# Attention block loop: the last weighted-value products issued before the third set of transposes, and the copy of their sum issued one iteration earlier

## The chip, the cores and the metric

The kernel runs on one core of a Trainium2 chip. The metric is the device time of one launch in microseconds (us), median of three runs. The engines are TensorE (PE, with its weight loads shown apart as PEld), VectorE (DVE), ScalarE (ACT), GpSimd (POOL) and SyncE (SP), which issues the DMAs.

## The reference

Three layers follow each other: a clustered attention, a bilinear layer and a gated layer. All inputs and outputs are float32.

```
q_assign = argmax(q_n . c_n);  k_assign = argmax(k_n . c_n)      # 16 clusters per head
scores   = q k^T / sqrt(64), masked to pairs of the same cluster
attn     = exp(scores - rowmax);  attn = attn / (rowsum + 1e-9)
x        = attn v                       # (2, 8, 768, 64) -> (1536, 512)
x        = ((x w1) * (x w2)) w3 w_out   # 512 -> 1024 -> 1024 -> 512
out      = (sigmoid(x w_gate) * (x w_val)) w_out2    # 512 -> 1536 -> 512
```

## The kernel before, in words

The attention runs over 16 heads as 8 pairs (`pr`), two heads (`e`) a pair and three groups of 256 queries (`q0`) a head: 48 blocks. One block goes through these steps, each of them a small function:

- `scores(j)`: for each half of the block (128 queries, j = 2i or 2i+1) four matmuls write 128 x 768 scores into PSUM (lines 312 to 315; pool `ps_s`, 2 buffers).
- `maxima(j)`: DVE takes the negated row maximum (`nm`, line 322). `exponentials(j)`: ACT writes exp(s + nm) to SBUF (`e`, line 333).
- `transposes(i, k2)`, k2 = 0, 1, 2: PE turns 256 of the 768 keys, four 128 x 128 transposes a set, into PSUM (`pt`, line 343; pool `ps_t`, 3 buffers).
- `split_hi` and `split_lo`: the turned weights are kept as a rounded part `ph` (ACT, line 361) and a remainder `pl` (DVE, line 372), which free the `pt` buffer. For half of the blocks the set k2 = 0 goes by ACT into `pc` (line 358), and POOL forms both parts.
- `weighted_v(i, k2)`: four matmuls (lines 384 and 385) add ph and pl times the values `vx` into `av`. The pool `ps_a` has a single buffer: one block's sum has to be copied out before the next block's first product may start.
- `take_x(i)`: ACT copies `av` into the pair's result `xa` (line 393).

The loop is software-pipelined: its iteration i issues scores for block i+1 or i+2, transposes for block i, and products for block i-1. From the start of the loop on, the instructions of PE, DVE, ACT, POOL and SP are issued in the order in which this code is written: there is no scheduler, and each engine takes its list from the front. `at` is the place of an iteration in its pair (0 to 5). Some iterations carry more: the preparation of the next pair (`prep_...`), the inverse of the row sums (`invert`, ACT line 407 and DVE line 408, at = 4) and its turn by PE (`turn_sums`, line 413, at = 5), and steps that convert the next layer's weights (`convert`; on ACT lines 93 and 94 or line 108), at the end of iterations at = 1 and 3, and in some pairs 5, of the pairs 1 to 6.

On PE an iteration is: four score matmuls, transposes 0, eight products (k2 = 0 and 1, of block i-1), four score matmuls, transposes 1, transposes 2, four products (k2 = 2). On ACT it is: `take_x(i-2)`, ph of set 2 of block i-1, ph or pc of set 0, an exponential, ph of set 1, a second exponential, and after it the conversion steps, if there are any.

After the attention the two matrix layers follow as one long list of matmuls (lines 65 to 67), with their evacuations attached. The last iterations of the attention, i = 47 to 49, drain it.

Of the kernel before, what the change touches and what calls it, by code (L numbers as in the profile page):

```python
# [27 lines left out]
def tile_cluster_attention__then__moe__then__gated_moe(  # L28
# [236 lines left out]
    def prep_code(pr):  # L265
        sm = opnd.pop((pr, "top"))
        lead(pr).tensor_tensor(out=sm, in0=sm, in1=dec.unsqueeze(1).broadcast_to([128, S // 32, C]), op=ALU.mult)
        opnd[pr, "code"] = sm
# [25 lines left out]
    def prep_v(pr, e):  # L294
        vx = core.tile([128, KT, 2, D], F32R, tag="vx", name=f"vx{pr}_{e}", bufs=3)
        split(raw[pr, "v"][:, e], vx[:, :, e, :], vx[:, :, 1 - e, :], nc.gpsimd, nc.gpsimd)
        opnd[pr, e, "v"] = vx
# [6 lines left out]
    def scores(j):  # L304

        if not 0 <= j < 2 * NB:
            return
        pr, e, q0 = blocks[j // 2]
        QH, KH, QX, KX = opnd[pr, e]
        q = slice(q0 + 128 * (j % 2), q0 + 128 * (j % 2) + 128)  # L310
        sp = ps_s.tile([128, 1024], F32, tag="s", name=f"s{j}")
        nc.tensor.matmul(sp[:, 0:512], QH[:, q], KH[:, 0:512], start=True, stop=False)
        nc.tensor.matmul(sp[:, 512:S], QH[:, q], KH[:, 512:S], start=True, stop=False)
        nc.tensor.matmul(sp[:, 0:512], QX[:, q], KX[:, 0:512], start=False, stop=True)
        nc.tensor.matmul(sp[:, 512:S], QX[:, q], KX[:, 512:S], start=False, stop=True)  # L315
        sps[j] = sp

    def maxima(j):
        if j not in sps:
            return  # L320
        nms[j] = core.tile([128, 1], F32, tag="nm", name=f"nm{j}", bufs=4)
        nc.vector.tensor_reduce(out=nms[j], in_=sps[j][:, 0:S], axis=AX.X, op=ALU.max, negate=True)  # L322
# [13 lines left out]
    def transposes(i, k2):  # L336
        if not 0 <= i < NB:
            return
        pt = ps_t.tile([128, 2, 256], F32, tag="t", name=f"pt{i}_{k2}")
        for kk in range(2):  # L340
            for t in range(2):
                k0 = 128 * (2 * k2 + kk)
                nc.tensor.transpose(pt[:, kk, 128 * t : 128 * t + 128], exps[2 * i + t][:, k0 : k0 + 128], ident)  # L343
        pts[i, k2] = pt

    def by_pool(i, k2):

        return k2 == 0 and i % 6 in (1, 2, 4)

    def split_hi(i, k2):  # L350
        if (i, k2) not in pts:
            return
        pt = pts[i, k2]
        ph = core.tile([128, 2, 256], F32R, tag="ph", name=f"ph{i}_{k2}", bufs=4)
        pl = core.tile([128, 2, 256], F32R, tag="pl", name=f"pl{i}_{k2}", bufs=4)
        if by_pool(i, k2):
            pc = core.tile([128, 2, 256], F32, tag="pc", name=f"pc{i}", bufs=1)
            nc.scalar.copy(pc, pt)
            pts[i, k2] = pc
        else:  # L360
            nc.scalar.copy(ph, pt)  # L361
        phs[i, k2] = (ph, pl)
# [11 lines left out]
    def weighted_v(i, k2):  # L374
        if not 0 <= i < NB:
            return
        pr, e, q0 = blocks[i]
        ph, pl = phs.pop((i, k2))
        if k2 == 0:
            avs[i] = ps_a.tile([128, 256], F32, tag="a", name=f"av{i}")  # L380
        for kk in range(2):
            kt = 2 * k2 + kk
            w = opnd[pr, e, "v"][:, kt].rearrange("p j d -> p (j d)")
            nc.tensor.matmul(avs[i], w, ph[:, kk, :], start=kt == 0, stop=False)  # L384
            nc.tensor.matmul(avs[i], w, pl[:, kk, :], start=False, stop=kt == KT - 1)  # L385

    def take_x(i):
        if i not in avs:
            return
        pr, e, q0 = blocks[i]  # L390
        if q0 == 0:
            acc_x[pr, e] = core.tile([128, S], F32, tag=f"xa{e}", name=f"xa{pr}_{e}", bufs=2 - e)
        nc.scalar.copy(acc_x[pr, e][:, q0 : q0 + 256], avs.pop(i))  # L393
# [16 lines left out]
    def turn_sums(pr):  # L410

        rp = ps_t.tile([128, 2, 256], F32, tag="t", name=f"rp{pr}")[0 : 2 * KT, 0, 0:128]
        nc.tensor.transpose(rp, acc_x.pop((pr, "sum")), ident)
        acc_x[pr, "rp"] = rp

    def store_sums(pr):
        rp = acc_x.pop((pr, "rp"))
        rt = core.tile([2 * KT, 128], F32, tag="rt", name=f"rt{pr}", bufs=1)
        nc.vector.tensor_copy(rt, rp)
        nc.sync.dma_start(r_dram[pr], rt)  # L420
# [85 lines left out]
    if True:  # L506
        for e in range(2):
            prep_v(0, e)
        for i in range(-2, NB + 2):
            pr, at = divmod(i, 6)  # L510
            nxt = pr + 1 if 0 <= i and pr + 1 < NPR else None
            later = nxt + 1 if nxt and nxt + 1 < NPR else None
            late = nxt == 1

            scores(2 * i + 3)
            take_x(i - 2)
            split_hi(i - 1, 2)
            transposes(i, 0)
            if i == NB - 1:
                turn_sums(pr)  # L520
            maxima(2 * i + 3)
            if i == NB - 1:
                store_sums(pr)
            if nxt and at == 1 + late:
                prep_code(nxt)
            if nxt and at == 1:
                prep_scatter(nxt, 1)
            if later and at == 0:
                load_qk(later)
            if at == 2 and 0 < pr and i < NB:  # L530
                join_x(pr - 1)
            split_lo(i - 1, 2)
            split_hi(i, 0)
            split_lo(i, 0)
            if nxt and at == 3:
                for e in range(2):
                    prep_mask(nxt, e)
            if 0 < pr and i < NB and at == 5:
                norm_x(pr - 1)
                split_x(pr - 1)  # L540
            if nxt and at == 2:
                prep_v(nxt, 0)
            if 0 < pr and i < NB and at == 3:
                add_x(pr - 1)
                spread(pr - 1, "xb", 1)
            exponentials(2 * i + 3)
            if later and at == 3:
                halves = prep_split(later)
                next(halves)
            if later and at == 4:  # L550
                for _ in halves:
                    pass
            weighted_v(i - 1, 0)
            weighted_v(i - 1, 1)
            if 0 <= i < NB - 1 and at == 5:
                turn_sums(pr)
            if i == 0:
                prep_scatter(1, 0)
            if later and at == 5:
                prep_scatter(later, 0)  # L560
            if at == 0 and pr < 4:
                convert(pr)

            scores(2 * i + 4)
            if nxt and at == 0 and not late or i == 1:
                prep_add(nxt)
            if 0 < pr < NPR and at == 0:
                prep_v(pr, 1)
            if nxt and at == 0:
                load_v(nxt)  # L570
            transposes(i, 1)
            split_hi(i, 1)
            transposes(i, 2)
            maxima(2 * i + 4)
            split_lo(i, 1)
            exponentials(2 * i + 4)
            weighted_v(i - 1, 2)
            if 0 <= i < NB and at == 4:
                invert(pr)
            if 0 <= i < NB - 1 and at == 5:  # L580
                store_sums(pr)
            if i == -2:
                halves = prep_split(1)
                next(halves)
            if i == -1:
                for _ in halves:
                    pass
            if i == 0:
                prep_sims(1)
                prep_sum(1)  # L590
            if nxt and at == late:
                prep_argmax(nxt)
            if nxt and at == 1 + late:
                prep_onehot(nxt)
            if nxt and at == 2:
                prep_turn(nxt)
            if (pr, at) in CONVERT:
                convert(CONVERT[pr, at])
            if later and at == 5:
                prep_sims(later)  # L600
                prep_sum(later)
            if i == NB - 2:
                end_move(0)
            if i == NB:
                end_move(1, FIRST)
                spread(END, "raw", 3)
                end_add(0)
        end_move(1, LAST)
        end_add(1, FIRST)
        end_norm(FIRST)  # L610
        end_split(FIRST)
        end_add(1, LAST)
        end_norm(LAST)
        end_split(LAST)
# [530 lines left out]
```

## Time and profile before

| | |
|---|---|
| median of 3 runs | 779.38 us (778.66 to 780.47) |
| the profiled execution, its own time | 780.68 us |
| its span, first to last instruction | 778.9 us |
| mean granted TensorE clock | 0.996 of full speed (2.4 GHz) |
| PE busy | 754.6 us (97%) |
| DVE, ACT, POOL busy | 575.4, 470.6, 410.8 us |
| first and last copy `xa<-av` of the attention | 32.66 and 254.19 us |
| first matmul of the layer after it | 253.99 us |

Times in the rows are counted from the start of the span. A row of the timeline gives start, duration, engine, line, operation, output and inputs. A bracket at its end gives the idle time of the engine before it and the instruction that ended it. Matmuls are pipelined, so the start of the next row, not the duration, tells how long one held the engine.

### The profile page before, as it was taken

The page shows a single profiled execution, that of the slowest core. Times are in us where ns is not written, and L with a number is a line of the kernel's source. Part 1 is how long each engine was busy: PE and PEld are TensorE (multiplying, and loading weights), DVE is VectorE, ACT ScalarE, POOL GpSimd, SP SyncE. Part 2 cuts the span into 40 slices and gives each one's busy share as a digit, 9 for nine tenths or more (in the row PEclk, how much of TensorE's full clock was granted, in tenths as well). Part 3 has the DMA queues.
Part 4 walks back from the last instruction along what each step waited for, and adds up shares of the span by engine and source line. Part 5 has one row for each costly group of instructions (what it writes and reads, how often), then busy time and mean ns, then how long its engine had stood idle before and what let it go on. Part 6 is the DMA issues. An engine that isn't in the chain of part 4 may idle for free.

```text
span 778.9 us, 12205 instructions
## 1 busy us (share of the span) xinstructions
PE 754.6 (97%) x4293; PEld 683.5 (88%) x4293; DVE 575.4 (74%) x895; ACT 470.6 (60%) x980; POOL 410.8 (53%) x418
## 2 busy tenths in 40 slices
PE   7999999998999999999999999899999999999998
PEld 7888888888988888888888999899999999999996
DVE  6798989898887566666673367658576877879674
ACT  3789788879787455546552244576756455564630
POOL 3447777776765256333241137474755647475520
PEclk9999999999999999999999999999999999999999
DMA  8867767666621534333340001130311213031004
GB/s 223 198 178 173 203 168 184 178 153 163 153 62 52 166 113 154 115 134 133 111 144 20 1 0 55 54 109 1 127 36 57 107 54 109 1 109 55 28 0 163
DMA packets 28893, 82.63 MB, mean 106 GB/s; under 512 B 4800, under 2 KB 4960, under 8 KB 28832
## 3 DMA queue, kind: packets, MB, share of 16 engines
q1 hardware_dynamic: 28832, 81.86, 35.7%
q8 instruction: 34, 0.56, 0.3%
q14 instruction: 27, 0.22, 0.1%
HBM read 52.49 MB, written 3.19 MB: 71 GB/s over the span
## 4 chain that ended last, share of the span: by engine, by line
PE 78%; DVE 6%; ACT 4%; issue 4%; DMA 3%; POOL 3%; SPq 2%; ACTq 0%; DVEq 0%; POOLq 0%
PE p L67 12%; PE p L66 12%; PE p L65 12%; PE p_a L65 4%; PE p_a L66 4%; PE p_a L67 4%; PE pt L343 4%; PE av L384 3%; PE av L385 2%; SPq L62 2%; PE p_b L65 2%; PE p_b L66 2%; PE p_b L67 2%; PE w34p L67 2%; PE w34p L65 2%
## 5 line engine op out<-in xcount | busy, mean ns | idle before, releaser
L322 DVE TENSOR_REDUCE nm<-s 128x1 f32<-128x768 f32 x96 | 90.3, 942 | 10.8 <-PE s L315 10.4
L333 ACT ACTIVATE e<-s,nm 128x768 f32<-128x768 f32 x96 | 87.4, 910 | 14.0 <-DVE nm L322 13.4
L384 PE MATMUL av<-ph,vx 128*128 128x256 f32 x288 | 80.6, 309 | 11.3 <-ACT xa L393 10.8
L372 DVE TENSOR_TENSOR pl<-pt,ph 128x512 fp32r<-128x512 f32 x120 | 80.0, 682 | 11.4 <-ACT ph L361 10.4
L361 ACT CAST ph<-pt 128x512 fp32r<-128x512 f32 x120 | 69.3, 594 | 23.4 <-PE pt L343 22.9
L343 PE MATMUL pt<-ident,e 128*128 128x128 f32 x576 | 79.8, 274 | 0.7 <-DVE pl L372 0.6
L65 PE MATMUL p<-x,w 128*128 128x512 f32 (+1 forms) x208 | 80.0, 385 | 0.0
L67 PE MATMUL p<-x,w 128*128 128x512 f32 (+1 forms) x208 | 80.0, 385 | 0.0
L66 PE MATMUL p<-x,w 128*128 128x512 f32 (+1 forms) x208 | 80.0, 385 | 0.0
L385 PE MATMUL av<-pl,vx 128*128 128x256 f32 x288 | 72.6, 281 | 0.0
L343 PEld LDWEIGHTS pt<-ident,e 128*128 128x128 f32 x576 | 67.3, 142 | 5.8 <-PE pt L343 0.9
L384 PEld LDWEIGHTS av<-ph,vx 128*128 128x128 f32 x288 | 54.3, 188 | 19.1 <-ACT xa L393 8.9
L106 POOL TENSOR_TENSOR w_a<-w_f 128x512 uint32<-128x512 uint32 x32 | 34.8, 1086 | 62.5 <-DVE w_f L105 28.6
L1024 DVE TENSOR_TENSOR acc<-p,acc 128x512 f32<-128x512 f32 x60 | 41.2, 687 | 29.9 <-PE p L67 29.5
L931 ACT COPY s<-p_a 128x384 f32<-128x384 f32 x72 | 34.4, 479 | 44.3 <-PE p_a L67 43.9
L855 POOL TENSOR_TENSOR wgv_a<-wgv_f 128x512 uint32<-128x512 uint32 x24 | 25.3, 1056 | 62.4 <-DVE wgv_f L854 43.7
L67 PE MATMUL p<-wo,u 128*128 128x512 f32 x144 | 57.0, 396 | 0.0
L66 PE MATMUL p<-wo,u 128*128 128x512 f32 x144 | 56.7, 394 | 0.0
L65 PE MATMUL p<-wo,u 128*128 128x512 f32 x144 | 56.0, 389 | 0.0
L385 PEld LDWEIGHTS av<-pl,vx 128*128 128x128 f32 x288 | 54.6, 190 | 0.1
L66 PEld LDWEIGHTS p<-x,w 128*128 128x128 f32 x208 | 39.1, 188 | 7.5
L67 PEld LDWEIGHTS p<-x,w 128*128 128x128 f32 x208 | 39.1, 188 | 7.5
(232 smaller groups left out, 2295.6 us busy)
## 6 DMA issues: line engine op xcount, KB each, us to landing
wgv_f<-in_w_gv_dram SPq DMA_DIRECT2D x24, 512.0 KB, 3.2
wo_f<-in_w_out_dram SPq DMA_DIRECT2D x20, 512.0 KB, 3.2
w_f<-in_w_dram SPq DMA_DIRECT2D x16, 512.0 KB, 4.3
w_f<-in_w3T_dram SPq DMA_DIRECT2D x16, 512.0 KB, 4.1
raw<-in_qkT_dram SPq DMA_DIRECT2D x16, 384.0 KB, 3.3
vraw<-in_v_dram SPq DMA_DIRECT2D x8, 384.0 KB
QH<-hi SPq DMA_DIRECT2D x16, 192.0 KB, 4.7
KH<-hi SPq DMA_DIRECT2D x16, 192.0 KB, 3.1
```

Source lines behind the costliest of these rows:

```text
L65: nc.tensor.matmul(ps, whi, xhi, start=start, stop=False, skip_group_check=more)
L66: nc.tensor.matmul(ps, whi, xlo, start=False, stop=False, skip_group_check=more)
L67: nc.tensor.matmul(ps, wlo, xhi, start=False, stop=stop, skip_group_check=more)
L106: nc.gpsimd.tensor_tensor(out=a, in0=high, in1=low, op=ALU.add)
L322: nc.vector.tensor_reduce(out=nms[j], in_=sps[j][:, 0:S], axis=AX.X, op=ALU.max, negate=True)
L333: nc.scalar.activation(et, sps.pop(j)[:, 0:S], AF.Exp, bias=nms.pop(j), accum_out=acc_x[pr, "sum"][:, at : at + 1])
L343: nc.tensor.transpose(pt[:, kk, 128 * t : 128 * t + 128], exps[2 * i + t][:, k0 : k0 + 128], ident)
L361: nc.scalar.copy(ph, pt)
L372: nc.vector.tensor_tensor(out=pl, in0=src, in1=ph, op=ALU.subtract)
L384: nc.tensor.matmul(avs[i], w, ph[:, kk, :], start=kt == 0, stop=False)
L385: nc.tensor.matmul(avs[i], w, pl[:, kk, :], start=False, stop=kt == KT - 1)
L1024: nc.vector.tensor_tensor(out=acc[:, t, :], in0=bk, in1=acc[:, t, :], op=ALU.add)
```

## The change

In each iteration of the attention loop the last four products of block i-1 (`weighted_v(i - 1, 2)`) move up on PE, from behind the transposes of set 2 of block i to in front of them. The copy of the finished sum moves on ACT from the head of the next iteration (`take_x(i - 2)` there) to the middle of the same one (`take_x(i - 1)`), behind the ph of set 1 and in front of the second exponential and of all that follows it.

```diff
             scores(2 * i + 3)
-            take_x(i - 2)
             split_hi(i - 1, 2)
             transposes(i, 0)
...
             transposes(i, 1)
             split_hi(i, 1)
+            weighted_v(i - 1, 2)
             transposes(i, 2)
+            take_x(i - 1)
             maxima(2 * i + 4)
             split_lo(i, 1)
             exponentials(2 * i + 4)
-            weighted_v(i - 1, 2)
             if 0 <= i < NB and at == 4:
                 invert(pr)
```

The lists of DVE, POOL and SP keep their order. Those of ACT and PE change in every iteration in the same way. ACT, in the iteration whose conversion steps are lines 93 and 94 (weights `w_1_0`; av_2259 is the sum of the block whose products end here, ph_2_2308 the last rounded part of the block after it), before:

```order
181 L333 ACTIVATE e_2257,ss_2050<-s_2223,nm_2237 128x768
182 L361 CAST ph_1_2278<-pt_1_2273 128x512
183 L333 ACTIVATE e_2289,ss_2050<-s_2268,nm_2286 128x768
184 L93 ACTIVATE w_1_0_a<-w_1_0_f_1274 128x512
185 L94 ACTIVATE w_1_0_f_1274<-w_1_0_f_1274 128x512
186 L393 COPY xa_0_2306<-av_2259 128x256
187 L361 CAST ph_2_2308<-pt_2_2281 128x512
188 L358 COPY pc_2325<-pt_0_2311 128x512
```

and the same place now:

```order
181 L333 ACTIVATE e_2257,ss_2056<-s_2224,nm_2237 128x768
182 L361 CAST ph_1_2278<-pt_1_2273 128x512
183 L393 COPY xa_0_2290<-av_2259 128x256
184 L333 ACTIVATE e_2295,ss_2056<-s_2268,nm_2292 128x768
185 L93 ACTIVATE w_1_0_a<-w_1_0_f_1274 128x512
186 L94 ACTIVATE w_1_0_f_1274<-w_1_0_f_1274 128x512
187 L361 CAST ph_2_2308<-pt_2_2285 128x512
188 L358 COPY pc_2325<-pt_0_2311 128x512
```

The copy has moved past an exponential and two conversion steps; the ph behind it stands at the same number as before. PE at the same place, from the second score group's last matmul to the next score group's first, before (`pt_1`, `pt_2` are the transposes of sets 1 and 2, `av_2259` the products):

```order
883 L343 MATMUL pt_1_2273<-ident,e_2175 128x128
884 L343 MATMUL pt_2_2281<-ident,e_2128 128x128
885 L343 MATMUL pt_2_2281<-ident,e_2175 128x128
886 L343 MATMUL pt_2_2281<-ident,e_2128 128x128
887 L343 MATMUL pt_2_2281<-ident,e_2175 128x128
888 L384 MATMUL av_2259<-ph_2_2229,vx_0_1874 128x256
889 L385 MATMUL av_2259<-pl_2_2230,vx_0_1874 128x256
890 L384 MATMUL av_2259<-ph_2_2229,vx_0_1874 128x256
891 L385 MATMUL av_2259<-pl_2_2230,vx_0_1874 128x256
892 L312 MATMUL s_2301<-KH_1_1788,QH_1_1787 128x512
```

and now:

```order
883 L343 MATMUL pt_1_2273<-ident,e_2175 128x128
884 L384 MATMUL av_2259<-ph_2_2229,vx_0_1874 128x256
885 L385 MATMUL av_2259<-pl_2_2230,vx_0_1874 128x256
886 L384 MATMUL av_2259<-ph_2_2229,vx_0_1874 128x256
887 L385 MATMUL av_2259<-pl_2_2230,vx_0_1874 128x256
888 L343 MATMUL pt_2_2285<-ident,e_2133 128x128
889 L343 MATMUL pt_2_2285<-ident,e_2175 128x128
890 L343 MATMUL pt_2_2285<-ident,e_2133 128x128
891 L343 MATMUL pt_2_2285<-ident,e_2175 128x128
892 L312 MATMUL s_2303<-KH_1_1788,QH_1_1787 128x512
```

The four products and the four transposes of set 2 have changed places; nothing else moved on PE.

## Rows read from the trace of the kernel before

**Rows 1.** The page's first part: busy time, share of the span and instructions by engine.

```profile
PE 754.6 (97%) x4293; PEld 683.5 (88%) x4293; DVE 575.4 (74%) x895; ACT 470.6 (60%) x980; POOL 410.8 (53%) x418
```

**Rows 2.** Busy time by stretch: PE, PEld, DVE, ACT, POOL, granted clock, DMA share, GB/s.

```profile
130.00:180.00 50.00, 47.05 (x342) 42.87 (x341) 45.37 (x65) 41.66 (x90) 38.59 (x35) 1.00 0.67 170
```

**Rows 3.** Waits from 25 to 255 us: who for whom, us, times, longest.

```profile
ACT ph L361 <- PE pt L343: 22.4, 32, 1.2
ACT e L333 <- DVE nm L322: 13.2, 27, 1.4
...
PE av L384 <- ACT xa L393: 10.8, 20, 1.3
...
DVE nm L322 <- PE s L315: 7.9, 22, 0.9
...
ACT xa L393 <- PE av L385: 1.9, 3, 1.4
...
PE pt L343 <- DVE pl L372: 0.6, 1, 0.6
```

**Rows 4.** Waits of PE from 255 us to the end, the longest.

```profile
PE p_a L65 <- ACT s L931: 2.0, 1, 2.0
```

**Rows 5.** Timeline of PE at the iteration with conversion lines 93 and 94.

```profile
149.93 0.60 PE L343 MATMUL pt<-ident,e 128*128 128x128 f32 x4
151.58 0.35 PE L384 MATMUL av<-ph,vx 128*128 128x256 f32 x1 [1.05 <-ACT xa L393]
...
153.30 1.04 PE L343 MATMUL pt<-ident,e 128*128 128x128 f32 x8
154.09 0.36 PE L384 MATMUL av<-ph,vx 128*128 128x256 f32 x1
...
154.65 0.39 PE L312 MATMUL s<-KH,QH 96*128 96x512 f32 x1
```

**Rows 6.** Timeline of ACT over the same iteration.

```profile
149.06 0.90 ACT L333 ACTIVATE e<-s,nm 128x768 f32<-128x768 f32 x1
...
149.95 0.67 ACT L93 ACTIVATE w_a<-w_f 128x512 f32<-128x512 f32 x1
150.51 0.68 ACT L94 ACTIVATE w_f<-w_f 128x512 uint32<-128x512 uint32 x1
151.06 0.38 ACT L393 COPY xa<-av 128x256 f32<-128x256 f32 x1
151.31 0.60 ACT L361 CAST ph<-pt 128x512 fp32r<-128x512 f32 x1
```

**Rows 7.** Timeline of DVE over the same iteration.

```profile
151.95 0.69 DVE L372 TENSOR_TENSOR pl<-pt,ph 128x512 fp32r<-128x512 f32 x1 [0.16 <-ACT ph L361]
153.50 0.96 DVE L322 TENSOR_REDUCE nm<-s 128x1 f32<-128x768 f32 x1 [0.86 <-PE s L315]
```

**Rows 8.** Timeline of PE: a transpose (line 413) between products and scores.

```profile
166.23 0.28 PE L385 MATMUL av<-pl,vx 128*128 128x256 f32 x1
166.35 0.27 PE L413 MATMUL rp<-ident,ss 128*12 128x128 f32 x1
...
166.69 0.28 PE L313 MATMUL s<-KH,QH 96*128 96x256 f32 x1
...
167.17 1.03 PE L343 MATMUL pt<-ident,e 128*128 128x128 f32 x8
```

**Rows 9.** Four of the 20 waits of PE for the copy, from its timeline.

```profile
63.26 0.36 PE L384 MATMUL av<-ph,vx 128*128 128x256 f32 x1 [1.05 <-ACT xa L393]
...
160.49 0.38 PE L384 MATMUL av<-ph,vx 128*128 128x256 f32 x1 [0.21 <-ACT xa L393]
165.32 0.36 PE L384 MATMUL av<-ph,vx 128*128 128x256 f32 x1 [0.42 <-ACT xa L393]
...
191.08 0.39 PE L384 MATMUL av<-ph,vx 128*128 128x256 f32 x1 [1.30 <-ACT xa L393]
```

**Rows 10.** Timeline of DVE at the iteration that takes the reciprocal of the row sums.

```profile
164.95 0.23 DVE L408 RECIPROCAL ss<-ss 128x12 f32<-128x12 f32 x1 [0.56 <-ACT ss L407]
...
165.91 1.27 DVE L372 TENSOR_TENSOR pl<-pt,ph 128x512 fp32r<-128x512 f32 x2
```

## The prediction

> **What bounds the kernel now.** I read the page's first part first: PE is busy 97% of the span, the others far less [rows 1]. Then the busy time by stretch: from 130 to 180 us, in the middle of the attention, PE is busy 47.05 of 50 us and DVE 45.37, so PE leads but not by much, and 2.95 us in each 50 are lost on it [rows 2]. The list of waits names the loss: from 25 to 255 us PE waited 10.8 us, 20 times, for the copy of the products' sum out of PSUM, and 0.6 us for anything else that has a row here [rows 3]. After the attention the longest wait of PE is one of 2.0 us [rows 4]. So what the attention gains on PE moves everything behind it forward, and 10.8 us is what this change can reach at most.
>
> Why PE waits is seen in one iteration. The four transposes of set 0 start at 149.93, and the first product, which needs the buffer of the sum, starts only at 151.58 after 1.05 us of idle time [rows 5]. ACT meanwhile runs an exponential at 149.06, then two conversion steps, and the copy comes at 151.06 [rows 6]. The sum was finished long before: its last products are those ahead of the scores. The wait is ACT's queue, not the copy.
>
> **The change part by part.** Nothing is added or removed; in each of 48 blocks four products change places with four transposes on PE, and one copy moves on ACT.
>
> *The copy.* It holds ACT for 0.25 us (151.06 to the next start at 151.31 [rows 6]) before as after. In front of the exponential and the conversions it delays these by at most 0.25 us, and the ph behind them, which it no longer precedes, starts where it did: 151.31. ACT's sum per block stays equal. The copy now waits for the four products. They are issued right behind the transposes that ph of set 1 waits for, and take 0.56 us to the next start plus 0.28 - 0.12 = 0.16 by which the last outlasts its step [rows 5, 8]; that ph keeps ACT for 0.60 us of this [rows 6]. So I cost the wait at nothing where ACT comes a little late, and at 0.72 - 0.60, some 0.1 us a block, where it does not.
>
> *PE in that iteration.* The transposes of set 0 end at 149.93 + 0.60 = 150.5, and the first product can start there instead of at 151.58, 1.05 us earlier. Eight products and four score matmuls take 153.30 - 151.58 = 1.72 us, so transposes 1 begin at 152.2 and, at half of 154.09 - 153.30 = 0.79 us, the moved products can begin at 152.6 [rows 5]. They need pl of set 2, which DVE forms from 151.95 to 152.64 behind a ph that has not moved [rows 7]: about 152.75, 0.15 us lost. Products (0.56) and transposes (0.4) end at 153.7, where the next scores stood at 154.65 [rows 5]: 0.95 us of 1.05 come back. DVE can follow: the maximum at 153.50 had been idle 0.86 us for these scores [rows 7].
>
> *Further on in this pair.* PE waited 0.21 and 0.42 us more at 160.49 and 165.32 [rows 9]. Both are gone when the copy stands earlier. But DVE is ahead by only its 0.86: the reciprocal at 164.95, which waits for ACT [rows 10], comes at 164.1, and the first pl after it, 0.65 of the 1.27 us from 165.91 [rows 10], is done at 166.56 - 0.86 = 165.7. It frees the buffer that transposes 1 need in this iteration, since the turned row sums take one of the three. PE could start them at 167.17 [rows 8] less 1.68 - 0.15 = 1.53, at 165.64, and waits to about 165.8: 0.16 lost. So of 1.05 + 0.21 + 0.42 = 1.68 us some 1.37 come back, 82%.
>
> *The moved order on PE.* It needs no new data: transposes 2 stood in that place, and their PSUM buffer is freed by the same pl that the products read; that wait showed 0.6 us in all [rows 3]. What is new is one step from products to transposes and one from transposes to scores per block. The trace has both around the turned sums: from 166.23 to 166.69 run a product (0.12, to 166.35), a transpose and a 512-column score matmul (0.24: the 0.48 us to 167.17 less two of 256 columns at 0.12), which leaves 0.10 for the transpose, what one takes in a run of eight (0.79 / 8) [rows 5, 8]. From transposes to products, which is there twice per iteration before as after, the first product takes 0.36 us and the others 0.28 [rows 5, 8]; 0.08 for each new step is the far bound, 2 x 48 x 0.08 = 7.7 us of loss. A gain is excluded: the step from products to scores that falls away cost nothing extra, since 0.56 us for four products is the first one's 0.20 and three steps of 0.12. I take 0, by the row that is the very step.
>
> *Sum.* 82% in the pair with large waits; where DVE has its own work after a small wait, less. With 80%: 10.8 x 0.8 = 8.6 us. The profiled execution took 780.68 us, so 772.1 of it; it lies 1.3 us above the median of the runs, so by the median 779.38 - 8.6 = 770.8 us.
>
> A check from the other side: DVE's idle time that scores ended is 7.9 us in 22 waits [rows 3]. DVE must run as much faster as PE does, and this is what it can take from PE; 8.6 is near it, and the rest has to come from its waits for ACT.
>
> **The rivals.**
>
> *A, DVE sets the pace (0.22).* For: DVE is busy 45.37 of 50 us [rows 2]; its list has long stretches without a pause, and there a PE that is early only waits for pl. Against: the idle time just named. Then only waits over 1 us, behind which DVE visibly idles, come back: there are four, 1.05, 1.30, 1.05 and 1.30 (the first at 63.26, the last at 191.08 [rows 9]), 4.7 us: 774.7 us. The Trainium skill, Perfetto Trace Analysis, section Identifying the Most-Contended Engine, has a rule that speaks for this: a PE's share of busy time is no good measure, its weight loads should be looked at, and the engine with the most occupancy is the one to relieve. Weight loads are busy 42.87 of 50 us here, under DVE's 45.37 [rows 2], so by that rule DVE comes first, and this change takes nothing off it.
>
> *B, the wait only moves (0.11).* The conversions still stand in front of ph of set 2, the moved products need it, and PE waits in front of them as it did for the copy. For: ph does not move (151.31), and its pl is done only at 152.64 [rows 6, 7]. Against: 1.72 us of products and scores lie between the old place of the wait and the new one. If all of it moved: 779.4 us.
>
> *C, slower: the copy at the head of ACT's queue (0.09).* The copy waits for products, these for pl, that for DVE, and behind the copy stands an exponential that was ready. If this is not covered, each block loses the copy's 0.25 us and 0.1 us of latency: 48 x 0.35 = 16.8 us, against 10.8 us won: 785.4 us. It decides from 10.8 / 48 = 0.225 us a block. For: only 27 of the 96 exponentials wait for their maximum long enough to have a row [rows 3]. Against: ACT idles 22.4 us for transposes [rows 3], and the head of the next iteration is free of the same copy. The Trainium skill, PSUM — Partial Sum Buffer, section Engine vs sequencer instructions, says that ScalarE's queue is strictly first in, first out, which is what this rival needs. The trace agrees: the copy at 151.06 starts behind both conversions although its sum was complete [rows 6].
>
> **How the numbers follow.** Forecast 0.58, A 0.22, B 0.11, C 0.09. A measurement of this kernel tells a change from none at about 0.2%, 1.6 us. Faster: forecast and A, 0.80; same: B, 0.11; slower: C, 0.09. The forecast's own range is 768.3 (all 10.8 us and a little at the drain) to 773.0 (60% of it). The range of 8 in 10 starts there, at 768.0, and reaches through A to 777.5, which leaves out B and C, 0.20.
>
> **What would show it.** In the list of waits PE for the copy falls from 10.8 us to under 1.5. New rows of PE for DVE's pl, at lines 384 and 385 or 343, come to 1 to 3 us. ACT's wait for the last product, 1.9 us [rows 3], grows to no more than 5. DVE's idle time for scores falls from 7.9 to about 3, and ACT's for maxima [rows 3] by some 3 us. The iteration with lines 93 and 94 shows its first product about 0.6 us behind the start of the transposes. The layer behind the attention takes as long as before. I am wrong if PE's wait for pl grows to 5 us or more (A or B), or if ACT's wait for products does (C).

## The result and the profile after

The changed kernel takes 773.65 us (median of 6 runs, 772.34 to 774.57) against 780.27 us of the kernel before (6 runs). The ratio is 0.9912, with a 95% interval of 0.990 to 0.9925: 6.9 us gained (5.9 to 7.8). The prediction was 770.8 us, a gain of 8.6, worked out from a median of 779.38 us before: the direction and the wait were right, the size was too large. The time lies in the range of 8 in 10 (768.0 to 777.5), but 0.65 us above the forecast's own (768.3 to 773.0), some 3 us from the forecast and 1 us from rival A's 774.7.

The page's first part, which answers to [rows 1]:

```profile
PE 752.9 (97%) x4293; PEld 683.8 (88%) x4293; DVE 577.3 (75%) x895; ACT 468.9 (61%) x980; POOL 409.8 (53%) x418
```

It hardly differs: the work is the same. What moved is seen in the list of waits from 25 to 250 us, which answers to [rows 3] (who for whom, us in all, times, longest; the window ends earlier because the attention does):

```profile
ACT e L333 <- DVE nm L322: 15.3, 25, 1.5
ACT ph L361 <- PE pt L343: 15.2, 23, 1.5
...
POOL xa L432 <- DMA xa<-xa: 8.3, 6, 2.2
...
PE av L385 <- DVE pl L372: 3.8, 6, 1.2
PE pt L343 <- DVE pl L372: 2.4, 6, 0.4
DVE nm L322 <- PE s L315: 2.4, 7, 0.5
...
ACT xa L393 <- PE av L385: 1.4, 1, 1.4
```

PE's 10.8 us for the copy are gone to the last; in their place stand 3.8 and 2.4 us for DVE's remainder pl. ACT's wait for the products did not grow (1.9 us before). The first matmul of the next layer starts at 248.09 us in place of 253.99. From there to the end it is 524.7 us, and was 524.9: the gain lies in the attention alone.

The iteration with conversion lines 93 and 94 on ACT, which answers to [rows 6]:

```profile
147.26 0.38 ACT L393 COPY xa<-av 128x256 f32<-128x256 f32 x1
147.52 0.93 ACT L333 ACTIVATE e<-s,nm 128x768 f32<-128x768 f32 x1
...
148.41 0.68 ACT L93 ACTIVATE w_a<-w_f 128x512 f32<-128x512 f32 x1
148.96 0.69 ACT L94 ACTIVATE w_f<-w_f 128x512 uint32<-128x512 uint32 x1
149.51 0.60 ACT L361 CAST ph<-pt 128x512 fp32r<-128x512 f32 x1
```

and on PE, which answers to [rows 5]:

```profile
148.13 0.60 PE L343 MATMUL pt<-ident,e 128*128 128x128 f32 x4
148.48 0.36 PE L384 MATMUL av<-ph,vx 128*128 128x256 f32 x1
...
150.22 0.60 PE L343 MATMUL pt<-ident,e 128*128 128x128 f32 x4
150.57 0.36 PE L384 MATMUL av<-ph,vx 128*128 128x256 f32 x1
150.90 0.39 PE L385 MATMUL av<-pl,vx 128*128 128x256 f32 x1
...
151.35 0.60 PE L343 MATMUL pt<-ident,e 128*128 128x128 f32 x4
151.71 0.48 PE L312 MATMUL s<-KH,QH 96*128 96x512 f32 x1
```

The first product follows the transposes at once. Of the four moved products the second, the first that needs pl, starts 0.33 us after the one ahead of it in place of 0.20: 0.13 us lost, where 0.15 had been reckoned. From transposes 0 to the next scores it is 3.58 us (148.13 to 151.71) and was 4.72 (149.93 to 154.65): 1.14 us came back.

What had not been reckoned comes some 6 us further on. DVE, POOL and PE there:

```profile
157.38 1.89 DVE L102 TENSOR_SCALAR w_a<-w_a 128x512 uint32<-128x512 uint32 x1
```

```profile
157.15 1.84 POOL L432 TENSOR_TENSOR xa<-xa,xb 128x768 f32<-128x768 f32 x1 [1.96 <-DMA xa<-xa]
```

```profile
160.79 0.39 PE L385 MATMUL av<-pl,vx 128*128 128x256 f32 x1 [1.22 <-DVE pl L372]
```

In the kernel before, the same two instructions of DVE and POOL do not overlap:

```profile
159.92 0.42 DVE L102 TENSOR_SCALAR w_a<-w_a 128x512 uint32<-128x512 uint32 x1
```

```profile
157.44 1.84 POOL L432 TENSOR_TENSOR xa<-xa,xb 128x768 f32<-128x768 f32 x1 [0.24 <-DMA xa<-xa]
```

DVE came 2.5 us earlier and POOL only 0.3, because POOL's addition of the two heads waits for a DMA that hardly moved. So DVE's conversion step runs into POOL's addition, takes 1.89 us for 0.42, and the pl behind it is late. The same happens at 128 us, to line 105 beside the addition that starts at 127.67; it took 0.68 us in the kernel before. DVE and PE there:

```profile
128.19 1.87 DVE L105 SCALAR_TENSOR_TENSOR w_f<-w_f,w_a 128x512 uint32<-128x512 uint32 x1
```

```profile
131.58 0.39 PE L385 MATMUL av<-pl,vx 128*128 128x256 f32 x1 [1.07 <-DVE pl L372]
```

The kernel before has such overlaps too, with another instruction of POOL: line 105 took 1.77 us at 80.97 and 1.78 at 169.28, beside POOL's line 59. DVE and POOL at the second:

```profile
169.28 1.78 DVE L105 SCALAR_TENSOR_TENSOR w_f<-w_f,w_a 128x512 uint32<-128x512 uint32 x1
```

```profile
168.66 1.84 POOL L59 TENSOR_TENSOR x<-xa,x 128x768 fp32r<-128x768 f32 x1
```

In the changed kernel these two steps take 2.20 and 1.12 us. So the change added two collisions to two that were there already.

### The profile page after: what moved, and what is told of

Its sections match the earlier page's. It is cut to its first block, busy times and chain, and to the rows that moved or that the text cites. A ratio compares the mean times of both kernels' runs of the same rounds, so it can differ in the third digit from the quotient of the medians.

```text
span 772.8 us, 12258 instructions
## 1 busy us (share of the span) xinstructions
PE 752.9 (97%) x4293; PEld 683.8 (88%) x4293; DVE 577.3 (75%) x895; ACT 468.9 (61%) x980; POOL 409.8 (53%) x418
## 4 chain that ended last, share of the span: by engine, by line
PE 79%; DVE 8%; ACT 6%; issue 3%; POOL 2%; DMA 1%; SPq 0%; ACTq 0%; DVEq 0%; POOLq 0%
PE p L66 12%; PE p L67 12%; PE p L65 12%; PE pt L343 4%; PE p_a L65 4%; PE p_a L66 4%; PE p_a L67 4%; ACT e L333 2%; PE av L385 2%; DVE nm L322 2%; PE av L384 2%; PE p_b L65 2%; PE p_b L66 2%; PE p_b L67 2%; ACT ph L361 2%
## 5 line engine op out<-in xcount | busy, mean ns | idle before, releaser
L343 PE MATMUL pt<-ident,e 128*128 128x128 f32 x576 | 87.3, 275 | 2.4 <-DVE pl L372 2.4
L385 PE MATMUL av<-pl,vx 128*128 128x256 f32 x288 | 74.7, 289 | 4.1 <-DVE pl L372 3.8
```

## The experiments

All ratios are to the kernel before, with 95% intervals; the changed kernel's is 0.9912 (0.990 to 0.9925).

**products_only**: the products move, the copy stays.

```diff
             split_hi(i, 1)
+            weighted_v(i - 1, 2)
             transposes(i, 2)
...
             exponentials(2 * i + 4)
-            weighted_v(i - 1, 2)
```

> Only the move on PE: the four last products stand in front of the transposes of set 2, the copy stays at the head of ACT's next iteration. If the copy's place in ACT's queue is what made PE wait, nothing is won: PE still waits about 10 to 11 us for the copy, ratio 0.998 to 1.002 against the kernel before. The rival, that the earlier products already free the buffer earlier: the wait falls to 6 us or less and the ratio is 0.995 or below.

Measured: 0.9994 (0.9985 to 1.0003), 779.69 us. PE still waits for the copy:

```profile
PE av L384 <- ACT xa L393: 10.5, 18, 1.3
```

The copy's place in ACT's queue is the wait; when the products end does not matter to it.

**copy_only**: the copy moves, the products stay behind transposes 2 (their line moves in the code, but not in PE's list).

```diff
-            take_x(i - 2)
...
             transposes(i, 2)
+            weighted_v(i - 1, 2)
+            take_x(i - 1)
...
             exponentials(2 * i + 4)
-            weighted_v(i - 1, 2)
```

> Only the move on ACT: the copy stands between ph of set 1 and the second exponential, the products stay behind the transposes of set 2. The copy's data then come 0.4 us later. If the place of the copy is the whole gain, PE's wait for the copy is gone, ACT waits some 0.3 us a block for products (10 to 14 us in all) where it would have waited for maxima anyway, and the ratio is 0.991 to 0.994. The rival, that the products have to move with it: the late exponentials hold up the loop, ratio 0.997 or above.

Measured: 0.994 (0.9926 to 0.9955), 775.65 us, at the upper end of what was expected of the theory. Waits of ACT for the products and of PE:

```profile
ACT xa L393 <- PE av L385: 9.2, 26, 1.4
...
PE pt L343 <- DVE pl L372: 4.3, 10, 1.2
```

The copy alone brings about two thirds. The move of the products, worth nothing by itself, is worth the rest here: it takes ACT's wait for them from 9.2 us to 1.4.

**copy_behind_exp**: PE as before; the copy behind the second exponential and ahead of the conversions and the inverse.

```diff
-            take_x(i - 2)
...
             exponentials(2 * i + 4)
             weighted_v(i - 1, 2)
+            take_x(i - 1)
```

> The order on PE is that of before; on ACT the copy stands behind the second exponential, but in front of the conversion steps and the inverse of the row sums. If these extra steps made the 20 waits, the large ones (over 1 us) are gone and PE's wait for the copy is under 2 us, ratio 0.991 to 0.994. The rival, that the exponential in front of the copy matters as much: the wait stays at 5 us or more, ratio 0.996 or above.

Measured: 0.997 (0.9959 to 0.9982), 778.24 us: the rival. PE's waits for the copy are 2.0 us under its own name and 5.6 us, 5 times, under the name of line 407, which on ACT stands right behind the copy. One of these, on PE and ACT:

```profile
106.54 0.35 PE L384 MATMUL av<-ph,vx 128*128 128x256 f32 x1 [1.45 <-ACT ss L407]
```

```profile
105.14 0.90 ACT L333 ACTIVATE e<-s,nm 128x768 f32<-128x768 f32 x1 [0.31 <-DVE nm L322]
...
106.03 0.36 ACT L393 COPY xa<-av 128x256 f32<-128x256 f32 x1
106.28 0.22 ACT L407 ACTIVATE ss<-ss 128x12 f32<-128x12 f32 x1
```

So the conversions were not the whole cause. An exponential in front ties the copy to DVE's maximum. At the same place PE waited 0.41 us, to 107.59, in the kernel before; here it waits 1.45, to 106.54. It came 2.09 us earlier and loses half of that again.

**join_early**: the changed kernel, with the joining DMAs at `at == 1`.

```diff
+            if at == 1 and 0 < pr and i < NB:
+                join_x(pr - 1)
             if nxt and at == 1:
                 prep_scatter(nxt, 1)
...
-            if at == 2 and 0 < pr and i < NB:
-                join_x(pr - 1)
```

> The changed kernel, with the three DMAs that join the two heads of a pair issued one iteration earlier (at = 1 in place of 2), which the earlier copy allows. Theory of the collision: GpSimd's addition (line 432) starts as soon as it may, some 2 us earlier, and no longer runs beside VectorE's conversion steps; lines 102 and 105 at 157 and 128 us take 0.42 and 0.7 us again in place of 1.89 and 1.87, PE's two waits for pl of 1.07 and 1.22 us shrink to under 0.2, and the time falls by 2.0 to 2.6 us, ratio to the kernel before 0.988 (the changed kernel 0.9912). The rival, that VectorE sets the pace at these places whatever GpSimd does: the two waits keep 0.6 us or more each, ratio 0.9905 to 0.992.

Measured: 0.9884 (0.9869 to 0.9899), 771.23 us. DVE and POOL at the place shown above:

```profile
155.02 0.42 DVE L102 TENSOR_SCALAR w_a<-w_a 128x512 uint32<-128x512 uint32 x1
```

```profile
152.91 1.84 POOL L432 TENSOR_TENSOR xa<-xa,xb 128x768 f32<-128x768 f32 x1
```

The addition waits for no DMA, ends 0.27 us before DVE's step, and the step takes 0.42 us. PE's waits of 1.07 and 1.22 us are gone; its wait for pl at line 385 falls from 3.8 to 1.7 us. The gain over the changed kernel is 0.0028 of 780 us, 2.2 us; the two intervals lie just apart. Only the two collisions with the addition are gone. Those of line 105 with POOL's line 59 are still there, 2.17 us each; the second:

```profile
163.97 2.17 DVE L105 SCALAR_TENSOR_TENSOR w_f<-w_f,w_a 128x512 uint32<-128x512 uint32 x1
```

**before_join**: the same edit on the kernel before, as a control.

> A control: the kernel before, with the three joining DMAs one iteration earlier and nothing else. There VectorE's lines 102 and 105 did not run beside GpSimd's line 432, so if the join's gain in the changed kernel is the end of a collision that the change made, nothing is won here: ratio 0.9985 to 1.0015. The rival, that earlier joins help by themselves (GpSimd waits less for DMAs): ratio 0.998 or below.

Measured: 1.0001 (0.9992 to 1.001). Earlier joins are worth nothing by themselves; they undo the collisions that the change added.

**turn_late**: the changed kernel, with the row sums' transpose behind transposes 2.

```diff
-            if 0 <= i < NB - 1 and at == 5:
-                turn_sums(pr)
...
             transposes(i, 2)
+            if 0 <= i < NB - 1 and at == 5:
+                turn_sums(pr)
             take_x(i - 1)
```

> The changed kernel, with PE's transpose of the row sums (line 413) moved behind the transposes of set 2 of the same iteration. The three buffers are then not one step out of turn where transposes 1 are issued. If the buffer makes the five waits of 0.43 us at line 343, they go, and with them the two for the reciprocal (0.6 us): the ratio falls by 0.002 to 0.004, to 0.987 to 0.989. The rival, that VectorE sets the pace there and PE waits for the same pl a few instructions later: waits of PE at line 385 grow by as much, ratio 0.990 to 0.992.

Measured: 0.9898 (0.9884 to 0.9911), 772.26 us, between the two expectations, its interval overlapping the changed kernel's: inconclusive by time. In the trace the waits at line 343 (2.4 us) are gone and those at line 385 go from 3.8 to 4.3 us, with both collisions of the addition still there (line 105 takes 1.83 us at 125.73, line 102 takes 2.02 at 154.63).

**join_turn**: both edits.

> Both edits on the changed kernel: the joining DMAs one iteration earlier and the row sums' transpose behind transposes 2. If the two losses are separate they add up: ratio 0.984 to 0.986, about 768.5 us. If VectorE sets the pace once one of them is gone: 0.987 to 0.9885, no better than the earlier join alone.

Measured: 0.985 (0.9836 to 0.9863), 768.86 us, apart from the interval of join_early: the fastest kernel here, 11.7 us below the kernel before. The two losses add up, and a little more; 0.9912 - 0.0028 - 0.0014 would be 0.987. Something else changed as well: lines 102 and 105 take 0.42 and 0.67 to 0.68 us at all their eight places in the attention, so the two overlaps with line 59 that join_early kept no longer stretch DVE. PE's waits that are left in its list:

```profile
PE s L312 <- ACT ph L361: 2.4, 2, 1.3
...
PE av L385 <- DVE pl L372: 0.9, 2, 0.7
...
PE s L312 <- ACT pc L358: 0.5, 1, 0.5
...
PE rp L413 <- DVE ss L408: 0.4, 1, 0.4
```

The first and the third are waits ahead of scores; ph and pc are only what ended last by then, since these scores do not read them.

**scatter_join_turn**: as join_turn, with the two blocks of DMAs of at = 1 in the other order on SyncE (operands first, then the join).

> As with both edits, but SyncE issues the six operand DMAs of the next pair's second head ahead of the joining DMAs of the same iteration, in place of behind them: the third joining DMA waits for the first two to land, and what stands behind it in SyncE's queue waits too. If that queue makes PE's last two long waits ahead of scores (0.54 and 1.28 us, by the times of issue the next pair's mask rows), they go: ratio 0.982 to 0.984 against 0.985. The rival, that the later join brings GpSimd's addition back beside lines 102 and 105: ratio 0.986 to 0.989.

Measured: 0.9894 (0.9875 to 0.9913), 772.09 us: the rival. The waits ahead of scores did go, which fits SyncE's queue as their cause. But the addition waits for its DMA again, and both collisions are back; DVE and POOL at the first:

```profile
127.29 2.23 DVE L105 SCALAR_TENSOR_TENSOR w_f<-w_f,w_a 128x512 uint32<-128x512 uint32 x1
```

```profile
127.13 1.84 POOL L432 TENSOR_TENSOR xa<-xa,xb 128x768 f32<-128x768 f32 x1 [2.56 <-DMA xa<-xa]
```

No order on PE, ACT, DVE or POOL differs from join_turn. These are the collisions put in and taken out by the time of DMAs alone, and they are worth 3.4 us here, net of the waits ahead of scores that went.

## Why the prediction was right, and where its size was off

- **What bounds the kernel** was right: PE in the attention, waiting for the copy. The wait went to zero, DVE's idle time for scores fell from 7.9 to 2.4 us (about 3 was forecast), and the rest of the kernel kept its time.
- **The copy at no cost** was right with the products moved (ACT waits 1.4 us for them, 1.9 before). copy_only shows what this rests on: with the products left behind transposes 2, ACT waits 9.2 us for them.
- **The iteration in detail** was right on ACT and a little low on PE: the exponential, the conversions and the copy hold ACT for 2.25 us in front of that ph, before (149.06 to 151.31) and after (147.26 to 149.51), and 0.13 us were lost at pl for 0.15. But 1.14 us came back for 0.95. The first product follows the transposes 0.35 us after their start; the 0.60 reckoned is the duration of their row, not the time that they hold PE.
- **The order on PE at nothing** was right: from transposes 1 to the next group's second 512-column matmul it was 153.30 to 155.00, 1.70 us, and is 146.08 to 147.77, 1.69 us, in the iteration before the one shown. Over all blocks products_only, with the new order and the old wait, took 0.9994.
- **The step that was mis-sized is the share of 80%**, the term "10.8 x 0.8 = 8.6 us"; measured is 6.9 / 10.8 = 64%. That is just above the 60% at which the forecast's own range ends; the time lies beyond that end because the kernel before now measures 780.27 us and not 779.38. The share rested on "DVE can follow", with DVE's instructions at the durations that they had; that line 105 took 0.68 us in one place and 1.78 in another was in the trace of before, and was not used. The runs showed two things in its place. First, two of them got longer, 0.42 to 1.89 and 0.68 to 1.87 us, beside POOL's addition; join_early gives back 2.2 us by removing just these two, and 6.9 + 2.2 = 9.1 is near the forecast. That an engine can be early and collide was not asked of DVE and POOL. Second, the out-of-turn buffer at the row sums cost 0.43 us in five pairs, 2.1 us in all, not 0.16. DVE and PE in one of them, in the changed kernel:

```profile
163.94 0.23 DVE L408 RECIPROCAL ss<-ss 128x12 f32<-128x12 f32 x1 [0.56 <-ACT ss L407]
```

```profile
164.31 0.27 PE L413 MATMUL rp<-ident,ss 128*12 128x128 f32 x1 [0.26 <-DVE ss L408]
...
165.71 0.63 PE L343 MATMUL pt<-ident,e 128*128 128x128 f32 x4 [0.43 <-DVE pl L372]
```

In each of the five pairs PE turns the row sums 0.37 to 0.38 us after the reciprocal's start, as soon as it may, where it was 1.40 us in this pair before (164.95 to 166.35). From the reciprocal on, DVE needs 1.77 to 1.78 us until transposes 1 can start, and PE 0.43 less. By the prediction PE was to gain 0.67 us on DVE there (1.53 less 0.86); it gained 0.88 (1.89 less 1.01). With the collisions of the addition out of the way, moving the row sums is worth 0.9884 - 0.985 = 0.0034, 2.7 us. How much of this is the buffer's was not separated: the same run also ends the two stretches of line 105 by line 59, and behind each of these PE waited 0.24 and 0.16 us in join_early.
- **Rival A** was partly right. PE's waits for pl came to 6.2 us, where 1 to 3 were forecast and 5 or more was the prediction's own sign of being wrong, and ACT's wait for maxima grew by 2.1 us where it was to fall by 3: DVE does set the pace in places. That the time still lay in the range owes something to the range's reaching through A. But more came back than its 4.7 us, and join_turn removes most of those waits without taking any instruction off DVE, so its amount of work was not the limit. **B** held for a small part: behind lines 93 and 94 PE waits for pl 0.12 to 0.34 us, where it waited 1.05 to 1.30 for the copy. **C** did not occur.
- **Not settled**: the listed waits of PE fall from 12.0 us (10.8, 0.6 and 0.6 in smaller rows) to 7.1 (3.8, 2.4 and 0.9), 4.9 us, while the layer behind starts 5.9 us earlier. The remaining 1.0 us has no row of its own. Whether the scores' last waits in join_turn are the mask rows' DMAs was not measured by itself.

## What to carry to other kernels

In an engine's fixed queue, put an instruction that frees a single buffer as early as its data allow, ahead of work that nobody awaits soon; and move what feeds it along, or the queue waits for that. When one engine is sped up, check which instructions of different engines will now run at the same time, above all where one of them is held to a DMA's time and cannot move along. A line that has two durations in one trace is a sign of such an overlap before any change is made. A control that undoes only the new overlap tells such a loss from a true limit of the engine.

## What the runs showed of the hardware

Some instructions of DVE and POOL on SBUF stretch each other. Line 102, 0.42 us alone, took 1.82 to 2.02 us when it began 0.11 to 0.32 us after POOL's addition (scatter_join_turn, the changed kernel, turn_late); in the changed kernel it ended at 159.27, 0.28 us after the addition's end at 158.99. Line 105, 0.68 us alone, ended 0.54 to 0.56 us after the end of POOL's instruction in each of its five stretches of over 1 us in the kernel before and the changed one, whichever of lines 432 and 59 that was. Two pl, which read PSUM, were not stretched: at 165.91 in the kernel before [rows 10] they took 1.27 us together, though POOL's line 436 ran from 165.82 to 167.66. The loser can be either engine. In join_turn, at 78 and 162 us, line 105 keeps its time and POOL's subtraction in line 59 takes 2.45 and 2.46 us in place of 1.84. DVE and POOL at the second:

```profile
162.16 0.67 DVE L105 SCALAR_TENSOR_TENSOR w_f<-w_f,w_a 128x512 uint32<-128x512 uint32 x1
```

```profile
162.08 2.46 POOL L59 TENSOR_TENSOR x<-xa,x 128x768 fp32r<-128x768 f32 x1
```

The Trainium skill, SBUF — State Buffer, section Who interferes with whom, says that DVE's second pair of SBUF ports is shared with GpSimd as an exclusive lock, and that whoever issues first keeps it. That one of the two is held whole agrees with these rows; that the first is spared agrees with line 102, but not with the last pair, where POOL started 0.08 us earlier by the trace and was the longer one.
